# Two direct tiles of batch 1's second layer become a quad of half-size products, in a schedule written by hand

## The chip, the cores and the metric

The kernel runs on one core of a Trainium2 chip. The engines are called as the profile calls them: PE (matmuls), PEld (its weight loads), DVE (vector), ACT (scalar), POOL and SP (the last mostly issues DMAs). The metric is the device time of one execution in microseconds (us); less is better.

## The reference

Four batches of block-sparse attention (8 heads, 768 positions, 64 channels per head, blocks of 32) are followed by a residual MLP over tokens and channels. Cut to what matters:

```python
scores = scale * np.matmul(q, k.transpose(0, 1, 3, 2))
scores = np.where(mask, scores, -1000000000.0)        # window, global and sampled blocks
attn = np.exp(scores - np.max(scores, axis=-1, keepdims=True))
attn = attn / (np.sum(attn, axis=-1, keepdims=True) + 1e-09)
x = np.matmul(attn, v)              # to [4, 768, 512], heads side by side
a1 = alpha1 * x + beta1
tok = np.einsum('ts,bsd->btd', w_tok, a1)              # 768 x 768 over tokens
u = x + lam * tok
a2 = alpha2 * u + beta2
ch = np.maximum(a2 @ w_ch1, 0.0) @ w_ch2               # 512 -> 2048 -> 512
out = u + lam * ch
```

The change touches the last product, `hidden @ w_ch2`, of batch 1: 768 tokens by 2048 hidden channels, times 2048 by 512.

## The kernel before

**Tiling.** Attention goes over 16 pairs of heads (four per batch). A pair is nine units; a unit is one piece of scores (PE, L601, into a PSUM tile), an exponential over it (ACT, L619, into `eT`), a multiplication by the 0/1 mask (DVE, L636), and the products with the values (PE, "PV", L648 and L671, into `op`). A finished pair is divided by its row sums (DVE, L688 and L689) into `x_sb`. POOL then scales `x_sb` for the token mix (L705, L706, `a1pp`), PE mixes tokens (L846), DVE adds (L858) and casts (`ubf`), a transposing DMA on SP's queue brings `ubf` to `uraw` (L898), and DVE scales that to `uT` (L889).

**The channel MLP.** The first layer goes by FFN rows (`job_f1`, L919): four matmuls of 384 columns into an `mm` tile, then a relu on ACT (L926) into one of 16 rows of `hts`. A batch has two halves of 384 tokens, so 32 rows; there are two buffers of `hts`. The second layer has six output tiles of 128 tokens per batch. A *direct* tile is `job_f2` (L1058): 16 matmuls of 512 columns in four jobs of four, into one `mm` tile, then one addition to `x_sb` (DVE, L1067) and a store on SP's queue.

**Quads.** Batches 2 and 3 (`STR = (2, 3)`) take some output tiles in twos, by Strassen's scheme in the form with shared sums: the two tiles are the rows, the two halves of the hidden channels the inner index, and the two halves of the 512 columns the output columns of a 2 × 2 block product. Seven products of half size (`job_p` calling `mul`, L1170: eight matmuls of 256 columns each) stand for the 32 matmuls of 512. They need four sums of activations (`job_s`, DVE, L1144), four differences of `w_ch2`'s quarters (`job_t`, DVE, L1098, 16 instructions in all, once for the kernel), and the accumulations (`plus`, DVE, L1180) into `x_sb`. Products that accumulate in one bank share it: 1, 6 and 5; 7 and 4; 2 and 3 in batch 3.

**PSUM.** Three rings of banks: `mm` (three buffers of one bank), `sp` (two buffers of two banks) and `op` (one). The ring order is that of allocation. A unit group takes two `mm` tiles and two `sp` tiles for its scores.

**Order of work.** After unit 45 the program is emitted from strings written by hand, `WEAVE = W1 + W2 + W2L + W3`, one string per group of three units. Each letter emits one job; the engines run what is emitted in order, each its own. The letters: `q` the scores of three units and the first exponential, `x` the next exponential, `k` the next mask multiplication, `p` the next PV, `f` an FFN row, `g` the next job of the second layer (a direct tile's quarter, or a product), `S` a sum of activations, `A` two rows of the weights' differences, `T` a piece of the token mix, `d` the transposing DMAs, `v` their scaling, `s` the start of a pair's mixing, `0 1 2` jobs of a plan, `K Q Y L` the loads and transpositions of the next pair. `g` and `S` take their jobs in the order of `P_ORDER` and `S_ORDER`. Groups are named p15 to p23 (`W1`), p24 to p35 (`W2`), p36 to p47 (`W2L`) and on. In the kernel before, batch 1 has six direct tiles in order, `A` stands in p29's end, p30 (W2[6]) and p33 (W2[9]).

Of the kernel before, what the change touches and what calls it, by code (L numbers as in the profile page):

```python
# [41 lines left out]
POUR = [-19, 2, 2]  # L42
W1 = [
# [9 lines left out]
]  # L53
W2 = [
# [12 lines left out]
]  # L67
W2L = [
# [18 lines left out]
]  # L87
STR = (2, 3)
HN = NH // 2
HC = DM // 2  # L90
FS = 6
# [157 lines left out]
def kernel(  # L249
# [16 lines left out]
    nc = tc.nc  # L266
# [194 lines left out]
    def sp_tile():  # L461
        return psum.tile([P, 2, 512], FP, name="sp", tag="sp", bufs=2)
# [111 lines left out]
    x_sbs = {}  # L574
# [234 lines left out]
    did = set()  # L809
# [3 lines left out]
    hts = {}  # L813
# [301 lines left out]
    def a_of(b, t, name, r=slice(0, HN)):  # L1115
        if name in ("X1", "X2"):
            return xs[(b, t, name)][:, r]
        c, half = {"11": (0, 0), "12": (0, 1), "21": (1, 0), "22": (1, 1)}[name]
        return hts[(b, c)][:, HN * half + r.start : HN * half + r.stop, ts(t, P)]

    SOP = {
        1: ("X1", "21", "22", ALU.add),
# [5 lines left out]
    def job_s(b, t, n, r=slice(0, HN)):  # L1128
        dst, a, c, op = SOP[n]
        rows = range(r.start, r.stop)  # L1130
        for name in (a, c):
            if name[0] == "X":
                assert all(("S", b, t, int(name[1]), m) in did for m in rows)
            else:
                h, half = divmod(int(name) - 11, 10)
                assert all(("f", b, h, HN * half + m) in did for m in rows)
        if n == 3:
            assert all(("S", b, t, 1, m) in did for m in rows)
        if n == 4:
            assert (b, t, 2) in did  # L1140
        if dst[0] == "X" and (b, t, dst) not in xs:
            tag, bufs = ("eT", 6) if b == B - 1 else ("xs", 4)
            xs[(b, t, dst)] = ap_.tile([P, HN, P], BF, name="xs", tag=tag, bufs=bufs)
        nc.vector.tensor_tensor(  # L1144
            out=a_of(b, t, dst, r), in0=a_of(b, t, a, r), in1=a_of(b, t, c, r), op=op
        )
        did.update(("S", b, t, n, m) for m in rows)
# [8 lines left out]
        7: ("21", "T3", 3),  # L1156
    }
    banks = {}

    def mul(b, t, n, ps, start, cols=slice(0, HC)):  # L1160
        a, m, need = PROD[n]
        assert m in bq or all((m, r) in did for r in range(0, HN, 2))
        if need:
            assert all(("S", b, t, need, r) in did for r in range(HN))
        c, half = {"1": (0, 0), "X": (1, 0)}.get(a[0], (1, 0))
        if need == 0:
            h, half = divmod(int(a) - 11, 10)
            assert all(("f", b, h, HN * half + r) in did for r in range(HN))
        for r in range(HN):
            nc.tensor.matmul(  # L1170
                ps,
                a_of(b, t, a)[:, r],
                b_rows(m, r)[:, 0, cols],
                start=(start and r == 0),
                stop=(r == HN - 1),
                skip_group_check=True,
            )

    def plus(x, ps):
        nc.vector.tensor_tensor(out=x, in0=x, in1=ps, op=ALU.add)  # L1180

    def twice(ps):
        return ps.unsqueeze(1).broadcast_to([P, 2, HC])

    lo, hi = slice(0, HC), slice(HC, DM)

    def job_p(b, t, n):
        x = x_sbs[b]
        last = (b, t) == (B - 1, NT // 2 - 1)
        bk = banks.setdefault((b, t), {})  # L1190
        if n in (1, 2, 7):
            bk[n] = sp_tile()[:, 0] if n == 1 else mm_tile()[:]
        if n == 3 and not last and 2 not in bk:
            bk[2] = mm_tile()[:]
        if n == 1:
            mul(b, t, 1, bk[1][:, lo], True)
            plus(x[:, t, lo], bk[1][:, lo])
        elif n == 2:
            mul(b, t, 2, bk[2][:, lo], True)
            if last or b < B - 1:  # L1200
                plus(x[:, t, lo], bk.pop(2)[:, lo])
            if last:
                emit_store(b, t, lo)
        elif n == 6:
            mul(b, t, 6, bk[1][:, lo], False)
            plus(x[:, t + 3, lo], bk[1][:, lo])
        elif n == 7:
            mul(b, t, 7, bk[7][:, lo], True)
            plus(x[:, t + 3, hi], bk[7][:, lo])
        elif n == 5:  # L1210
            mul(b, t, 5, bk[1][:, lo], False)
            plus(x[:, t : t + 4 : 3, hi], twice(bk[1][:, lo]))
        elif n == 4:
            mul(b, t, 4, bk[7][:, lo], False)
            plus(x[:, t + 3, lo], bk[7][:, lo])
            emit_store(b, t + 3, slice(0, DM))
        elif last:
            for h in range(2):
                sl = slice(HC + h * P, HC + h * P + P)
                ps = (mm_tile(), op_tile([P, DM]))[h]  # L1220
                mul(b, t, 3, ps[:, sl], True, ts(h, P))
                plus(x[:, t, sl], ps[:, sl])
                emit_store(b, t, sl, (nc.sync, nc.scalar)[h])
        else:
            sl = hi if b < B - 1 else slice(0, DM)
            mul(b, t, 3, bk[2][:, hi], b < B - 1)
            plus(x[:, t, sl], bk[2][:, sl])
            emit_store(b, t, slice(0, DM))
        did.add((b, t, n))

    NPAIR = B * NP
# [34 lines left out]
    def start_mlp(b):  # L1266
# [4 lines left out]
        else:  # L1271
            todo["f"] += [
                lambda c=c, n=n: job_f1(b, c, n) for c in range(2) for n in range(NH)
            ]
        if b not in STR:
            todo["g"] += [
# [6 lines left out]
        ]  # L1283
        todo["S"] += [lambda t=t, n=n, r=r: job_s(b, t, n, r) for t, n, r in S_ORDER[b]]

    REST = (6, 7, 5, 4, 3)
    P_ORDER = {
        2: [(0, g, "g") for g in range(4)]
        + [(t, 2) for t in (1, 2)]
        + [(3, g, "g") for g in range(4)]  # L1290
        + [(t, 1) for t in (1, 2)]
        + [(t, n) for t in (1, 2) for n in REST],
        3: [(t, n) for t in range(2) for n in (1, 2)]
        + [(t, n) for t in range(2) for n in REST]
        + [(2, n) for n in (1, 2) + REST],
    }
    ALL, R1, R2 = slice(0, HN), slice(0, HN // 2), slice(HN // 2, HN)
    S_ORDER = {
        2: [(t, n, ALL) for t in (1, 2) for n in (1, 2, 3, 4)],
        3: [(t, n, R1) for n in (1, 2, 3) for t in range(3)]  # L1300
        + [(t, n, r) for t in range(3) for n, r in ((1, R2), (2, R2), (3, R2), (4, ALL))],
    }

    def start_pair(i):
# [227 lines left out]
```

## Time and profile before

| | |
|---|---|
| median of 3 runs | 298.71 us (298.64 to 299.35) |
| profiled execution | 298.76 us, span 297.1 us |
| granted PE clock | 1.000 |
| busy PE | 289.7 us (98%) |
| busy PEld | 193.5 us (65%) |
| busy DVE | 237.8 us (80%) |
| busy ACT | 217.1 us (73%) |
| busy POOL | 109.8 us (37%) |
| second layer, direct (L1058) | 205 records of 128x512 |
| half-size products (L1170) | 128x256, four groups by tile |

The span is from the first instruction to the last; the execution's time adds what lies around it. A row of a group gives line, engine, operation, tiles, count, then busy time and mean duration of one in nanoseconds, then the engine's idle time ahead and what ended it. Matmuls are pipelined: a matmul's duration is longer than its spacing to the next. In a timeline row stand start and length of a stretch of like instructions, in us, their count, and in brackets how long the engine had been idle and what released it. A window row gives the busy time of each engine in that stretch, the PE clock, the DMA share and GB/s.

### The profile page before, as it was taken

What the parts mean: (1) busy time and instruction counts of PE and PEld (TensorE: products, weight loads), DVE (VectorE), ACT (ScalarE), POOL (GpSimd) and SP (SyncE); (2) the same over time, 40 slices, a digit from 0 to 9 for tenths busy, and PEclk for the clock granted to TensorE, in tenths of its full rate; (3) what the DMA queues carried; (4) which work ended last, traced back from release to release, by engine and by line L of the source; (5) the groups of instructions that cost most, each with busy time, mean ns of one, the idle gap of its engine ahead of it and who ended that gap; (6) DMA issues with size and microseconds to landing.
All of it is one profiled execution on the core that took longest, in us unless ns stands there. A gap on an engine that the chain in (4) does not pass through costs nothing.

```text
span 297.1 us, 7554 instructions
## 1 busy us (share of the span) xinstructions
PE 289.7 (98%) x3082; PEld 193.5 (65%) x3101; DVE 237.8 (80%) x485; ACT 217.1 (73%) x324; POOL 109.8 (37%) x149
## 2 busy tenths in 40 slices
PE   8999999999999999999999999999999999999995
PEld 3688888665567565565576466556576679665884
DVE  4988899995678796977878777895956899799774
ACT  4999999998899963999779581999869744576000
POOL 8997978632443710355323340335320300000000
PEclk9999999999999999999999999999999999999999
DMA  6999999992392995729955767745520211400032
GB/s 182 184 199 186 192 171 187 171 123 44 95 147 55 112 203 84 118 65 119 125 96 73 124 110 146 103 92 69 70 62 17 38 38 29 141 1 3 0 141 73
DMA packets 57274, 31.09 MB, mean 105 GB/s; under 512 B 37204, under 2 KB 54016, under 8 KB 57240
## 3 DMA queue, kind: packets, MB, share of 16 engines
q0 software_dynamic: 16752, 14.22, 34.4%
q1 hardware_dynamic: 40020, 15.92, 29.3%
q8 instruction: 24, 0.39, 0.6%
q10 hardware_dynamic: 468, 0.47, 0.5%
q14 instruction: 10, 0.08, 0.1%
HBM read 29.75 MB, written 6.29 MB: 121 GB/s over the span
## 4 chain that ended last, share of the span: by engine, by line
PE 84%; DVE 6%; DMA 4%; ACT 3%; issue 1%; POOL 1%; SPq 0%; POOLq 0%
PE mm L919 18%; PE mm L1058 13%; PE sp L601 10%; PE mm L846 8%; PE op L671 7%; PE mm L1170 5%; PE sp L1170 4%; PE mm L601 3%; DVE eT L636 3%; PE mm L822 3%; PE op L648 2%; DMA vr<-in_v_dram 2%; ACT eT L619 2%; PE mm L1016 2%; PE sp L1016 2%; DMA uraw<-ubf 2%
## 5 line engine op out<-in xcount | busy, mean ns | idle before, releaser
L619 ACT ACTIVATE eT<-sp,expb 128x1024 f16<-128x1024 f32 x111 | 118.4, 1120 | 2.1 <-PE sp L601 1.4
L636 DVE TENSOR_TENSOR eT<-eT,mask 128x1024 f16<-128x1024 f16 x99 | 80.6, 843 | 13.5 <-ACT eT L619 13.3
L919 PE MATMUL mm<-uT,w1b 128*128 128x384 bf16 x416 | 76.8, 326 | 0.4 <-ACT hts L926 0.3
L705 POOL TENSOR_TENSOR a1pp<-x_sb,vbc 128x384 bf16<-128x384 f32 x25 | 28.5, 1138 | 119.0 <-DVE x_sb L689 84.7
L619 ACT ACTIVATE eT<-mm,expb 128x512 f16<-128x512 f32 x66 | 41.7, 685 | 26.5 <-PE mm L601 26.3
L926 ACT ACTIVATE hts<-mm 128x384 bf16<-128x384 f32 x104 | 49.1, 502 | 13.3 <-PE mm L919 12.4
L919 PEld LDWEIGHTS <-w1b 128*128 128x128 bf16 x416 | 38.7, 98 | 26.4 <-issue 2.9
L1058 PE MATMUL mm<-w2b,hts 128*128 128x512 bf16 x205 | 52.2, 379 | 0.9 <-issue 0.2
L671 PEld LDWEIGHTS <-eT 128*128 128x128 f16 x792 | 29.8, 98 | 8.8 <-issue 1.7
L1058 PEld LDWEIGHTS <-hts 128*128 128x128 bf16 x224 | 19.8, 98 | 22.3 <-issue 3.9
L671 PE MATMUL op<-vext,eT 128*128 128x65 f16 x792 | 32.1, 194 | 0.4 <-DVE x_sb L689 0.3
L601 PE MATMUL sp<-qTs,kTs 88*128 88x512 bf16 (+1 forms) x120 | 26.9, 325 | 1.2 <-ACT eT L619 0.7
L706 POOL TENSOR_TENSOR a1pp<-a1pp,vbc 128x384 bf16<-128x384 bf16 x25 | 26.7, 1069 | 2.0
L846 PE MATMUL mm<-a1pp,wtokT 128*128 128x256 bf16 x216 | 25.9, 273 | 0.1
L846 PEld LDWEIGHTS <-wtokT 128*128 128x128 bf16 x216 | 20.6, 98 | 5.6 <-issue 1.8
L1170 PEld LDWEIGHTS <-hts 128*128 128x128 bf16 x208 | 19.5, 98 | 3.0 <-issue 0.3
L858 DVE TENSOR_TENSOR x_sb<-x_sb,mm 128x512 f32<-128x512 f32 x18 | 12.3, 686 | 9.9 <-PE mm L846 9.8
L601 PE MATMUL sp<-qhT,khT 64*128 64x256 bf16 (+1 forms) x176 | 19.8, 322 | 0.0
L601 PEld LDWEIGHTS <-khT 64*128 64x128 bf16 x264 | 10.6, 94 | 12.7 <-issue 9.2
L648 PEld LDWEIGHTS <-eT 128*128 128x128 f16 x360 | 14.9, 97 | 3.8 <-issue 0.3
L689 DVE TENSOR_TENSOR x_sb<-op,rcp 128x384 f32<-128x384 f32 x28 | 15.6, 558 | 1.0
L1067 DVE TENSOR_TENSOR x_sb<-x_sb,mm 128x512 f32<-128x512 f32 x14 | 9.6, 686 | 8.2 <-PE mm L1058 6.7
(135 smaller groups left out, 376.9 us busy)
## 6 DMA issues: line engine op xcount, KB each, us to landing
out_dram<-x_sb SPq DMA_DIRECT2D x23, 256.0 KB
qpad<-in_q_dram POOLq DMA_DIRECT2D x15, 192.0 KB, 4.6
kr<-in_k_dram POOLq DMA_DIRECT2D x15, 192.0 KB, 5.3
vr<-in_v_dram POOLq DMA_DIRECT2D x15, 192.0 KB, 6.3
w1b<-in_moe_w_ch_dram POOLq DMA_DIRECT2D x4, 512.0 KB, 9.2
w2b<-in_moe_w_ch_dram POOLq DMA_DIRECT2D x4, 512.0 KB, 7.7
hts<-in_moe_w_tok_dram POOLq DMA_DIRECT2D x2, 576.0 KB, 8.7
x_sb<-in_k_dram ACTq DMA_DIRECT2D x2, 192.0 KB
```

What stands on the lines that cost most here:

```text
L601: nc.tensor.matmul(sp[jj][:, dst], lhsT, rhs, start=True, stop=True, skip_group_check=True,)
L619: nc.scalar.activation(dst, at, AF.Exp, bias=expb[:], scale=SCALE)
L636: nc.vector.tensor_mul(out=e, in0=e, in1=keep)
L648: nc.tensor.matmul(op[0][:, o, :], ets[u][:, jj, h * QB + n * P : h * QB + n * P + P], vexts[i % NVB][:, w, 2 * jp + jj, :], start=op[1] == 0,
L671: nc.tensor.matmul(op[0][:, o, :], ets[u][:, jj, h * QB + n * P : h * QB + n * P + P], vexts[i % NVB][:, w, 2 * jp + jj, :], start=op[1] == 0,
L705: eng.tensor_tensor(out=dst, in0=x_sbs[b][:, :, cols], in1=bc[0], op=ALU.mult)
L706: eng.tensor_tensor(out=dst, in0=dst, in1=bc[1], op=ALU.add)
L846: nc.tensor.matmul(ps[:, o], wtokT[:, os_, ts(2 * n + o, P)], a1pps[i][:, os_, :], start=(os_ == 0 and o == 0), stop=(os_ == NT - 1 and o ...
L919: nc.tensor.matmul(ps[:, 0:QC], w1b[:, dk, ts(n, P)], uTs[b][:, dk, ts(c, QC)], start=(dk == 0), stop=(dk == 3),)
L926: nc.scalar.activation(h_row(b, c, n), ps[:, 0:QC], AF.Relu)
L1058: nc.tensor.matmul(ps[:], ht[:, nk, ts(o % 3, P)], w2b[:, nk, :], start=(nk == 0), stop=(nk == NH - 1),)
L1170: nc.tensor.matmul(ps, a_of(b, t, a)[:, r], b_rows(m, r)[:, 0, cols], start=(start and r == 0), stop=(r == HN - 1), skip_group_check=True,)
```

## The change

Batch 1's tiles 0 and 1 become a quad; its tiles 2 to 5 stay direct and follow it. `STR` includes batch 1, the order of its second layer is products 2, 1, 6, 5, 7, 3, 4 and then the direct tiles. Tiles of a quad are now given as a pair `(o1, o2)`, since 0 and 1 are not three apart as the pairs of batches 2 and 3 are. Batch 1's product 1 takes an `mm` tile (kept through 6 and 5) in place of an `sp` tile, and product 3 has an `mm` tile of its own. The 16 differences move from p29, p30 and p33 into seven groups of `W1` and the first of `W2`. The FFN rows of batch 1 move forward: p30 has nine in place of seven, p31 six in place of four, and p34, p35 and p36 have none of their two, one and one left. The jobs of the second layer move back. `W2L` and `W3` are the same. The number of sums in `S` rises by four, each over eight rows (128x1024).

```diff
 W1 = [
     "q x L 0 k p f 1 2 f f x p f f f k p K f k",
-    "q Y 0 f 1 k p 2 x f f f x f k k p f g",
+    "q Y 0 f 1 k A A A p 2 x f f f x f k k p f g",
     "q x g f f x 0 k 1 p k g 2 Q k",
-    "q K x g p k 0 k 1 x Q p L Y f f g 2 g k",
-    "q g g x x 0 1 f k 2 k f p k p",
-    "q 0 s 1 s k x x p T f 2 k f k p",
+    "q A A K x g p k 0 k 1 x Q p L Y f f g 2 g k",
+    "q A A A g g x x 0 1 f k 2 k f p k p",
+    "q A A A 0 s 1 s k x x p T f 2 k f k p",
     "q 0 Q 1 k T p x Y k 2 x f p k K",
-    "q f 0 1 x s f T 2 f L d k k x f k f p p",
-    "q 0 x p x g k k 1 d g k g 2",
+    "q f 0 1 x s f T 2 f L d k A k x f k f p p",
+    "q A A 0 x p x g k k 1 d g k g 2",
 ]
 W2 = [
-    "q 0 p p g k x L x p f k 1 K 2 k",
+    "q A A 0 p p g k x L x p f k 1 K 2 k",
...
-    "q k 0 f x f p s f f x 1 L p k 2 f f f k Y A A A A A f",
-    "q f L f 0 f k A A A A A A A A 1 f Y x f p g x f p f g k k 2",
-    "q x k x k Q 0 g 1 s f f g p 2 p f f k p",
-    "q T 0 k f 1 x k f T x f 2 p k K p",
-    "q A A A x 0 x T k 1 k f 2 k f Q f d p L",
-    "q x 0 x K k g d k s f g f 1 k p p g 2",
-    "q Y g x x k g k f 0 1 k 2 p g v g v",
+    "q k 0 f x f p s f f x 1 L p k 2 f f f k Y f",
+    "q f L f 0 f k 1 f f S Y x f p f x f p f k k 2",
+    "q x f k x f k Q 0 1 s f f p 2 p f f k S p",
+    "q T 0 k f 1 x k f T x f 2 p k K p g",
+    "q S S g x 0 x T k g 1 k f 2 k f Q f d p L",
+    "q x 0 x K k g d k s g 1 k p p g 2",
+    "q Y g x x k g k 0 1 k 2 p g v g v",
 ]
...
-STR = (2, 3)
+STR = (1, 2, 3)
...
+    LATE = [(2, (1, 4)), (2, (2, 5))] + [(3, (o, o + 3)) for o in range(3)]
...
     def job_p(b, t, n):
-        x = x_sbs[b]
-        last = (b, t) == (B - 1, NT // 2 - 1)
+        x, (o1, o2) = x_sbs[b], t
+        tail = b == B - 1
+        last = tail and o2 == NT - 1
         bk = banks.setdefault((b, t), {})
-        if n in (1, 2, 7):
-            bk[n] = sp_tile()[:, 0] if n == 1 else mm_tile()[:]
-        if n == 3 and not last and 2 not in bk:
-            bk[2] = mm_tile()[:]
+        if n == 1 and (b, t) in LATE:
+            bk[1] = sp_tile()[:, 0]
+        elif n in (1, 2, 7) or (n == 3 and not tail):
+            bk[n] = mm_tile()[:]
...
+    def direct(*tiles):
+        return [(o, g, "g") for o in tiles for g in range(4)]
+
+    def quad(t, order):
+        return [(t, n) for n in order]
...
     P_ORDER = {
+        1: quad((0, 1), (2, 1, 6, 5, 7, 3, 4)) + direct(2, 3, 4, 5),
...
     S_ORDER = {
+        1: [((0, 1), n, ALL) for n in (1, 2, 3, 4)],
```

What the diff leaves out replaces the arithmetic on one tile number by the pair of tiles, in `a_of`, `mul` and the rest of `job_p`, gathers the checks of readiness in `a_ready`, and writes batches 2 and 3's orders, which stay the same, with `quad` and `direct`. In the changed kernel's numbering `mul`'s matmul is L1169, `plus` L1179 and the sums L1145.

More of the change, by code (lines that the diff above doesn't have):

```diff
@@ L1117, in a_of, with a_ready @@
             return xs[(b, t, name)][:, r]
-        c, half = {"11": (0, 0), "12": (0, 1), "21": (1, 0), "22": (1, 1)}[name]
-        return hts[(b, c)][:, HN * half + r.start : HN * half + r.stop, ts(t, P)]
+        o, half = t[int(name[0]) - 1], int(name[1]) - 1
+        return hts[(b, o // 3)][:, HN * half + r.start : HN * half + r.stop, ts(o % 3, P)]
+    def a_ready(b, t, name, rows):
+        if name[0] == "X":
+            return all(("S", b, t, int(name[1]), m) in did for m in rows)
+        o, half = t[int(name[0]) - 1], int(name[1]) - 1
+        return all(("f", b, o // 3, HN * half + m) in did for m in rows)
     SOP = {
@@ L1130, in job_s @@
         rows = range(r.start, r.stop)
[L1131 to L1136, printed above, removed]
+        assert a_ready(b, t, a, rows) and a_ready(b, t, c, rows)
         if n == 3:
@@ L1164, in mul @@
             assert all(("S", b, t, need, r) in did for r in range(HN))
[L1165 to L1168, printed above, removed]
+        assert a_ready(b, t, a, range(HN))
         for r in range(HN):
@@ L1221, in job_p @@
                 mul(b, t, 3, ps[:, sl], True, ts(h, P))
-                plus(x[:, t, sl], ps[:, sl])
-                emit_store(b, t, sl, (nc.sync, nc.scalar)[h])
-        else:
[L1225 to L1228, printed above, removed]
+                plus(x[:, o1, sl], ps[:, sl])
+                emit_store(b, o1, sl, (nc.sync, nc.scalar)[h])
+        else:
+            assert {(b, t, m) for m in (1, 2, 5)} <= did
+            sl, ps = (slice(0, DM), bk[2]) if tail else (hi, bk[3])
+            mul(b, t, 3, ps[:, hi], not tail)
+            plus(x[:, o1, sl], ps[:, sl])
+            emit_store(b, o1, slice(0, DM))
         did.add((b, t, n))
@@ L1284, in start_mlp @@
         todo["S"] += [lambda t=t, n=n, r=r: job_s(b, t, n, r) for t, n, r in S_ORDER[b]]
+    def direct(*tiles):
+        return [(o, g, "g") for o in tiles for g in range(4)]
+    def quad(t, order):
+        return [(t, n) for n in order]
     REST = (6, 7, 5, 4, 3)
     P_ORDER = {
[L1288 to L1295, printed above, removed]
+        1: quad((0, 1), (2, 1, 6, 5, 7, 3, 4)) + direct(2, 3, 4, 5),
+        2: direct(0)
+        + quad((1, 4), (2,))
+        + quad((2, 5), (2,))
+        + direct(3)
+        + quad((1, 4), (1,))
+        + quad((2, 5), (1,))
+        + quad((1, 4), REST)
+        + quad((2, 5), REST),
+        3: quad((0, 3), (1, 2))
+        + quad((1, 4), (1, 2))
+        + quad((0, 3), REST)
+        + quad((1, 4), REST)
+        + quad((2, 5), (1, 2) + REST),
     }
     ALL, R1, R2 = slice(0, HN), slice(0, HN // 2), slice(HN // 2, HN)
+    Q3 = [(0, 3), (1, 4), (2, 5)]
     S_ORDER = {
-        2: [(t, n, ALL) for t in (1, 2) for n in (1, 2, 3, 4)],
-        3: [(t, n, R1) for n in (1, 2, 3) for t in range(3)]
-        + [(t, n, r) for t in range(3) for n, r in ((1, R2), (2, R2), (3, R2), (4, ALL))],
+        1: [((0, 1), n, ALL) for n in (1, 2, 3, 4)],
+        2: [(t, n, ALL) for t in ((1, 4), (2, 5)) for n in (1, 2, 3, 4)],
+        3: [(t, n, R1) for n in (1, 2, 3) for t in Q3]
+        + [(t, n, r) for t in Q3 for n, r in ((1, R2), (2, R2), (3, R2), (4, ALL))],
     }
```

19 lines of the change are left out of this document (10 added, 9 removed).

## The prediction

> **What bounds the kernel now.** I read the page's share of each engine and its chain first, then a table by stage over the groups that the change touches, then timelines at their seams.
>
> ```profile
> PE 289.7 (98%) x3082; PEld 193.5 (65%) x3101; DVE 237.8 (80%) x485; ACT 217.1 (73%) x324; POOL 109.8 (37%) x149
> PEclk9999999999999999999999999999999999999999
> PE 84%; DVE 6%; DMA 4%; ACT 3%; issue 1%; POOL 1%; SPq 0%; POOLq 0%
> ```
>
> PE is busy for 98% of the span at full clock and holds 84% of the chain that ended last. The table below has a row per group, from the group's first score matmul to the next one's; I write p30 for the group whose text is W2[6], so p34 is W2[10] and p36 is W2L[0].
>
> ```profile
> 134.56:142.44 7.88, 7.83 (x69) 4.49 (x70) 6.16 (x18) 6.76 (x12) 3.40 (x6) 1.00 1.17 141
> 142.44:148.73 6.29, 6.24 (x70) 3.81 (x70) 5.08 (x6) 4.79 (x8) 2.56 (x2) 1.00 1.01 122
> 154.89:159.38 4.49, 4.49 (x47) 3.08 (x45) 3.90 (x10) 4.09 (x8) 0.00 (x0) 1.00 0.00 0
> 159.38:164.88 5.50, 5.45 (x55) 2.94 (x54) 5.26 (x8) 4.42 (x7) 3.83 (x5) 1.00 0.86 115
> 164.88:170.21 5.33, 5.17 (x41) 2.55 (x42) 3.49 (x8) 3.66 (x5) 0.67 (x2) 1.00 0.89 157
> 170.21:173.69 3.48, 3.43 (x54) 2.11 (x54) 2.17 (x4) 3.06 (x4) 3.40 (x5) 1.00 0.05 6
> sum 56.63, PE 56.21 PEld 34.53 DVE 44.57 ACT 41.83 POOL 20.25; mean PE 6.25 PEld 3.84 DVE 4.95 ACT 4.65 POOL 2.25
> ```
>
> Columns: the stretch, its length, then busy PE, PEld, DVE, ACT, POOL. The sum is over nine groups, 127.77 to 184.40 (three not shown). PE is busy for 56.21 of 56.63 us: no wait to remove, so only fewer PE microseconds gain, and each new wait of PE is paid in full. ACT is the runner-up: 6.76 of 7.88 us in p30.
>
> **The change part by part.** *Fewer matmul columns.* Two direct tiles (32 matmuls of 512 columns) become seven products (56 of 256).
>
> ```profile
> 174.44 1.90 PE L1058 MATMUL mm<-w2b,hts 128*128 128x512 bf16 x8
> 232.02 1.04 PE L1170 MATMUL mm<-w2b,hts 128*128 128x256 bf16 x8
> 135.32 3.42 PE L919 MATMUL mm<-uT,w1b 128*128 128x384 bf16 x20
> L1058 PE MATMUL mm<-w2b,hts 128*128 128x512 bf16 x205 | 52.2, 379 | 0.9 <-issue 0.2
> L1170 PE MATMUL mm<-w2b,hts 128*128 128x256 bf16 (+1 forms) x80 | 10.0, 267 | 0.0
> L919 PE MATMUL mm<-uT,w1b 128*128 128x384 bf16 x416 | 76.8, 326 | 0.4 <-ACT hts L926 0.3
> ```
>
> A run of eight takes seven pitches and one duration: (1.90 − 0.379)/7 = 0.217 us at 512 columns, (1.04 − 0.267)/7 = 0.110 at 256; at 384, (3.42 − 0.326)/19 = 0.163. 32 × 0.217 = 6.94 and 56 × 0.110 = 6.16: −0.78 us, all on PE.
>
> The Trainium skill ("TensorE: Matmul & The Clock Gate", section "Back-to-back issue gap") gives about 131 ns for a sustained matmul of 512 columns and 81 for one of 128; by an estimate midway, 98 ns at 256, the quad would cost 56 × 0.098 = 5.5 against 32 × 0.131 = 4.2, or +1.3 us. The two first rows say otherwise (217 and 110 ns), so the sum stays with them.
>
> *Sixteen weight differences (L1098) leave p30 (13) and p33 (3) for the first ten groups.*
>
> ```profile
> 134.42 1.41 DVE L1098 TENSOR_TENSOR qTs<-w2b 128x512 bf16<-128x512 bf16 x4
> L1098 DVE TENSOR_TENSOR qTs<-w2b 128x512 bf16<-128x512 bf16 x4 | 1.4, 409 | 0.0
> 66.25 0.69 DVE L636 TENSOR_TENSOR eT<-eT,mask 128x1024 f16<-128x1024 f16 x1 [0.31 <-ACT eT L619]
> 67.46 0.53 PE L671 MATMUL op<-vext,eT 128*128 128x65 f16 x12
> 75.65 0.69 DVE L1067 TENSOR_TENSOR x_sb<-x_sb,mm 128x512 f32<-128x512 f32 x1 [0.87 <-PE sp L601]
> 82.00 0.69 DVE L1067 TENSOR_TENSOR x_sb<-x_sb,mm 128x512 f32<-128x512 f32 x1 [2.10 <-PE mm L1058]
> 85.66 0.69 DVE L636 TENSOR_TENSOR eT<-eT,mask 128x1024 f16<-128x1024 f16 x1 [1.16 <-ACT eT L619]
> 99.18 0.20 DVE L688 RECIPROCAL rcp<-op 128x6 f32<-128x6 f32 x1 [0.87 <-PE op L671]
> 104.23 0.69 DVE L1067 TENSOR_TENSOR x_sb<-x_sb,mm 128x512 f32<-128x512 f32 x1 [0.94 <-PE mm L1058]
> ```
>
> One costs DVE about 0.335 us ((1.41 − 0.409)/3, with 0.409 the mean of that row's group), 5.4 for all. Each new place stands at a DVE idle time (in brackets): three in p16 where 0.31 is idle, two in p18 at 0.87, three in p19 at 2.10, three in p20 at 1.16, two in p23 at 0.87, two in p24 before 0.94; the single one of p22 has no row here. Only the first overflows, by 3 × 0.335 − 0.31 = 0.70, and its mask product is done at 66.25 + 0.69 = 66.94, 0.5 before the PV that reads it, so 0.2 would show. I take 0, since five of six places hold what they get. Bounds: 0, and 0.7 at each of three places should the idle time lie elsewhere (2.1). Where the differences leave, PE had no wait, so nothing returns. What fills p30's DVE instead is less (6.16 busy falls by about 4), and it doesn't matter.
>
> *Four sums (L1145) and seven accumulations instead of two.*
>
> ```profile
> L1144 DVE TENSOR_TENSOR hts<-hts,xs 128x1024 bf16<-128x1024 bf16 x5 | 3.4, 684 | 0.0
> L1180 DVE TENSOR_TENSOR x_sb<-x_sb,sp 128x512 f32<-128x512 f32 x5 | 3.4, 684 | 0.5 <-PE sp L1170 0.5
> L1180 DVE TENSOR_TENSOR x_sb<-x_sb,mm 128x256 f32<-128x256 f32 x15 | 6.2, 417 | 1.4 <-PE mm L1170 1.4
> ```
>
> These are batch 2's and 3's (by form). Sums 4 × 0.68, accumulations 6 × 0.42 + 0.68 less 2 × 0.69: +4.5 us of DVE in p30 to p37, which has 44.57 busy of 56.63. Free in itself; its queueing is priced in the fourth wait. ACT's relus are the same in number, only earlier; POOL and SP issue the same DMAs, and SP stores batch 1's first two tiles once a product has ended, behind the transposing DMAs, with no reader.
>
> *FFN rows move forward.* p30 goes from 7 rows to 9, p31 from 4 to 6, p34 from 2 to 0, p35 and p36 from 1 to 0; second-layer jobs take their places. PE's sum is unchanged by it, but ACT's and the three `mm` banks' timing isn't. I follow each bank from its user to its next taker.
>
> ```profile
> 158.47 1.27 ACT L926 ACTIVATE hts<-mm 128x384 bf16<-128x384 f32 x3
> 171.79 2.12 ACT L619 ACTIVATE eT<-sp,expb 128x1024 f16<-128x1024 f32 x2
> 170.63 1.27 ACT L619 ACTIVATE eT<-mm,expb 128x512 f16<-128x512 f32 x2 [1.67 <-PE mm L601]
> 159.38 0.40 PE L601 MATMUL mm<-qhT,khT 64*128 64x512 bf16 x2
> 173.91 0.60 PE L601 MATMUL sp<-qhT,khT 64*128 64x256 bf16 x6
> ```
>
> Relus back to back are 0.385 apart and last 0.50; wide exponentials 1.0 apart, 1.12 long; half ones 0.58 apart.
>
> - Wait 1, start of p31. Its second score tile takes the bank of the eighth of p30's nine FFN rows. In p30 ACT has, from the fifth relu on (its matmuls end 4.2 us into the group): relu 0.38, exponential 1.0, relus 0.38 and 0.38, exponential 1.0, relu 0.49: it ends at 7.83. PE arrives at p30's length of 7.88 with two rows more and two jobs of four 512s fewer: 7.88 + 2 × 0.65 − 8 × 0.217 = 7.44. **+0.4** (0.2 to 0.55).
> - Wait 2, in p31: its fourth row takes the bank of its first, whose relu stands behind an exponential on ACT: 0.37 + 2 × 0.58 + 1.0 + 0.50 = 3.03 into the group, where PE has done its scores (0.87) and three rows: 0.87 + 3 × 0.65 = 2.82. **+0.2** (0 to 0.4).
> - Wait 3, start of p34. Products 1, 6 and 5 hold one `mm` bank, so the score tile waits for the last FFN relu of p33 and no longer for the one before. The row of three relus ends at 159.74, PE arrives at 159.38: 0.36, less up to 0.1 for the tile's place within its pair: **+0.28** (0.2 to 0.4).
> - Wait 4, start of p35. The second score tile takes the bank of product 3, whose eight matmuls are the last of p34; before, a direct tile's bank stayed open across the seam. DVE must add it first.
>
> ```profile
> 161.10 3.35 DVE L636 TENSOR_TENSOR eT<-eT,mask 128x1024 f16<-128x1024 f16 x3 [0.21 <-ACT eT L619]
> 167.31 1.99 DVE L636 TENSOR_TENSOR eT<-eT,mask 128x1024 f16<-128x1024 f16 x3
> 160.97 1.00 POOL L705 TENSOR_TENSOR a1pp<-x_sb,vbc 128x384 bf16<-128x384 f32 x1 [9.22 <-DVE x_sb L689]
> 162.05 1.25 POOL L706 TENSOR_TENSOR a1pp<-a1pp,vbc 128x384 bf16<-128x384 bf16 x1
> ```
>
> With DVE idle: the last matmul's duration beyond its pitch (0.267 − 0.110) and the add's 0.417, **0.57**. But p34's DVE has three mask products, 3.35 us while POOL computes against 1.99 without, and now two further additions ahead of it: by this the backlog is 0.6 more, **+1.17**; with a second stretched product 1.9. I take 1.17, since those POOL operations come at this place. The Trainium skill ("SBUF — State Buffer", "Who interferes with whom") has the two share a port with exclusive use, which these rows bear out.
>
> - Wait 5, p36 to p37. Without its FFN row p36 is 0.65 us shorter for PE (4 × 0.163), while ACT still has four exponentials from 170.63 to 171.79 + 2.12 = 173.91, and PE's scores into `sp` began at 173.91, of which the second tile, 0.2 later, takes the bank of the last exponential. 0.65 − 0.2: **+0.45** (0.3 to 0.5).
>
> Cover gone at each: the FFN matmuls that stood between a relu and the next score tile. After p37 the program is as before.
>
> Sum: −0.78 + 0 + 0.4 + 0.2 + 0.28 + 1.17 + 0.45 = +1.72. The profiled execution took 298.76 with its span of 297.1, 0.05 above the median 298.71. Forecast 298.71 + 1.72 = **300.4 us**.
>
> **The rivals.**
>
> - *No new wait (the other side).* One condition decides: DVE and ACT are done with a bank when PE comes to it at every seam, as in all of the shown groups before, where PE lost 0.42 in nine. For it: ACT is busy for only 41.83 of 56.63 us, DVE for 44.57. Against: the walks above are by order, not by load. Time 298.71 − 0.78 = 297.9.
> - *Waits at their low ends.* DVE is idle when product 3 ends and the rest absorb one another: −0.78 + 0.2 + 0 + 0.2 + 0.57 + 0.3 = +0.49, or 299.2. From p30 on DVE loses 4 us of differences, which speaks for it.
> - *The early differences delay the mask products.* Three places are overrun by the 0.7 of the first, which keeps 0.2 after its PV's margin while the two others keep 0.5 each: 300.4 + 1.2 = 301.6. Against: the idle times above.
> - *Half-size matmuls are no cheaper.* A pitch above 6.94/56 = 0.124 us turns the gain around; a tenth of a 512's 0.217 above half of it, 0.130, would make +0.3 instead of −0.78: 301.5. The 0.110 row speaks against.
>
> **How the numbers follow.** Forecast 0.50 (own range 299.6 to 301.2), low ends 0.20, no wait 0.10, early differences 0.12, half-size 0.03, something not seen 0.05. The forecast, the low ends and the early differences hold 0.82, so the range goes from the low ends less 0.3 to 301.7, a little over the early differences: 298.9 to 301.7. No change is what lies within 0.3% (0.9 us; about what a measurement can tell): 297.8 to 299.6. Forecast: slower 0.48, same 0.02. Low ends: same 0.17, slower 0.03. No wait: same 0.06, faster 0.04. Early differences and half-size: slower 0.15. Unseen: faster 0.02, same 0.01, slower 0.02. Together faster 0.06, same 0.26, slower 0.68.
>
> **What would show it.** The pitch of products in p32 to p35 at 0.110; no PE wait before 130 us and DVE idle shorter at the six places; PE waits with releaser ACT `hts` at the starts of p31 and p34, DVE `x_sb` (L1180's successor) at p35, and ACT `eT` at p37. Wrong if the p35 wait is under 0.6 (low ends) or if PE waits on DVE `eT` in the first ten groups.

## The result and the profile after

The changed kernel takes 299.80 us (median of 5 runs, 299.72 to 300.55) against 298.70 us before (298.62 to 299.35). The ratio of the runs is 1.0049 with a 95% interval of 1.0037 to 1.0062: slower, and by 1.1 us between the medians. The forecast was 300.4 in a range of 298.9 to 301.7. The profiled execution took 299.72 with a span of 298.0, against 298.76 and 297.1. One execution of all that follow (306.47 us in run 9, at a granted clock of 0.989) is left out of the medians and ratios.

The first table is the groups p29 to p37 of the changed kernel (five of the nine rows and their sum), each from its first score matmul to the next one's (length, then busy PE, PEld, DVE, ACT, POOL); the rows answer to those of the prediction, with the new start times.

```profile
134.54:141.98 7.44, 7.44 (x69) 4.47 (x68) 2.26 (x5) 6.72 (x13) 3.37 (x5) 1.00 1.12 144
141.98:148.50 6.52, 6.39 (x69) 3.97 (x68) 5.48 (x7) 6.22 (x13) 2.61 (x2) 1.00 1.14 115
161.87:166.35 4.48, 4.48 (x59) 3.48 (x57) 3.62 (x8) 3.50 (x5) 3.43 (x4) 1.00 0.79 95
166.35:171.71 5.36, 4.96 (x42) 2.65 (x42) 3.78 (x9) 3.27 (x4) 0.96 (x2) 1.00 1.07 194
171.71:174.53 2.82, 2.82 (x49) 1.85 (x48) 2.06 (x4) 2.40 (x4) 2.31 (x3) 1.00 0.10 32
sum 58.06, PE 57.22 PEld 37.25 DVE 42.22 ACT 41.96 POOL 20.29; mean PE 6.36 PEld 4.14 DVE 4.69 ACT 4.66 POOL 2.25
```

The nine groups take 58.06 us in place of 56.63: +1.43, while their first matmul stands at 127.75 in place of 127.77. So everything ahead of them, with the 16 differences in it, costs nothing. A busy PE isn't a PE at work: the two score matmuls at 141.98, one of which waits for a bank, read 0.83, the two at 155.55 0.39. So the waits are read from the spacing of the rows. At a seam without a wait the next job starts 0.75 us after the first score matmul (155.55 to 156.30 below).

PE's rows of the changed kernel at the seams (start, length, tiles, count):

```profile
141.98 0.83 PE L601 MATMUL mm<-qhT,khT 64*128 64x512 bf16 x2
143.18 2.99 PE L919 MATMUL mm<-uT,w1b 128*128 128x384 bf16 x16
146.01 0.90 PE L671 MATMUL op<-vext,eT 128*128 128x65 f16 x24
...
155.55 0.39 PE L601 MATMUL mm<-qhT,khT 64*128 64x512 bf16 x2
...
156.30 1.05 PE L1169 MATMUL mm<-w2b,hts 128*128 128x256 bf16 x8
...
161.87 0.65 PE L601 MATMUL mm<-qhT,khT 64*128 64x512 bf16 x2
...
162.89 1.05 PE L1169 MATMUL mm<-qTs,xs 128*128 128x256 bf16 x8
...
165.39 1.04 PE L1169 MATMUL mm<-w2b,hts 128*128 128x256 bf16 x8
166.35 0.28 PE L601 MATMUL mm<-qhT,khT 64*128 64x256 bf16 x1
167.03 0.38 PE L601 MATMUL mm<-qhT,khT 64*128 64x256 bf16 x3 [0.40 <-DVE x_sb L1179]
...
167.77 1.05 PE L1169 MATMUL mm<-kTs,hts 128*128 128x256 bf16 x8
...
174.53 0.39 PE L601 MATMUL mm<-qhT,khT 64*128 64x512 bf16 x2
...
175.46 0.39 PE L601 MATMUL sp<-qhT,khT 64*128 64x512 bf16 x2 [0.31 <-ACT eT L619]
175.78 1.90 PE L1058 MATMUL mm<-w2b,hts 128*128 128x512 bf16 x8
```

All five waits are there: p31 starts 143.18 − 141.98 − 0.75 = 0.45 late; its first four rows take 146.01 − 143.18 = 2.83 in place of 2.60 (16 pitches of 0.163), so 0.23; p34 loses 162.89 − 161.87 − 0.75 = 0.27; p35 167.77 − 166.35 − 0.75 = 0.67; p37 175.78 − 174.53 − 0.75 = 0.50. In sum 2.12. With −0.78 that is +1.34 of the +1.43 measured; the last 0.09 I can't place. A product of eight has the length 1.05, the 1.04 of the kernel before.

Behind p37 some of it comes back. The rows are p38 to p40 together, of the kernel before and then of the changed one:

```profile
sum 12.34, PE 11.98 PEld 6.40 DVE 10.12 ACT 10.70 POOL 3.93; mean PE 3.99 PEld 2.13 DVE 3.37 ACT 3.57 POOL 1.31
```

```profile
sum 11.92, PE 11.92 PEld 6.49 DVE 10.32 ACT 10.69 POOL 4.23; mean PE 3.97 PEld 2.16 DVE 3.44 ACT 3.56 POOL 1.41
```

0.42 us less: in the kernel before a PV in p40 waits, behind a division on DVE, for a scaling that waits for its transposing DMA. The first fence below is the kernel before, the second the changed one.

```profile
192.81 0.48 DVE L889 TENSOR_SCALAR uT<-uraw,ab2T 128x768 bf16<-128x768 bf16 x1 [0.62 <-DMA uraw<-ubf]
195.25 0.91 PE L671 MATMUL op<-vext,eT 128*128 128x65 f16 x24 [0.25 <-DVE x_sb L689]
```

```profile
193.14 0.86 DVE L889 TENSOR_SCALAR uT<-uraw,ab2T 128x768 bf16<-128x768 bf16 x2
196.24 0.90 PE L671 MATMUL op<-vext,eT 128*128 128x65 f16 x24
```

1.43 − 0.42 = 1.01, and the profiled executions differ by 0.96.

### The profile page after: what moved, and what is told of

It is laid out like the page before. It is cut to its first block, busy times and chain, and to the rows that moved or that the text cites. A ratio compares the mean times of both kernels' runs of the same rounds, so it can differ in the third digit from the quotient of the medians.

```text
span 298.0 us, 7632 instructions
## 1 busy us (share of the span) xinstructions
PE 291.4 (98%) x3125; PEld 196.2 (66%) x3125; DVE 241.3 (81%) x494; ACT 217.1 (73%) x324; POOL 109.7 (37%) x149
## 4 chain that ended last, share of the span: by engine, by line
PE 86%; ACT 6%; DVE 4%; issue 1%; DMA 1%; ACTq 0%
PE mm L919 21%; PE mm L1058 13%; PE sp L601 11%; PE mm L846 8%; PE op L671 7%; PE mm L1169 6%; ACT eT L619 4%; PE sp L1169 4%; PE mm L601 3%; PE mm L822 3%; PE op L648 2%; PE mm L1016 2%; PE sp L1016 2%; DVE eT L636 2%; PE mm L648 1%; ACT hts L926 1%
## 5 line engine op out<-in xcount | busy, mean ns | idle before, releaser
L636 DVE TENSOR_TENSOR eT<-eT,mask 128x1024 f16<-128x1024 f16 x99 | 79.5, 828 | 14.6 <-ACT eT L619 14.5
L705 POOL TENSOR_TENSOR a1pp<-x_sb,vbc 128x384 bf16<-128x384 f32 x25 | 28.5, 1139 | 120.1 <-DVE x_sb L689 86.2
L1058 PE MATMUL mm<-w2b,hts 128*128 128x512 bf16 x192 | 46.6, 380 | 0.0
L1058 PEld LDWEIGHTS <-hts 128*128 128x128 bf16 x192 | 17.0, 97 | 18.7 <-issue 2.8
L706 POOL TENSOR_TENSOR a1pp<-a1pp,vbc 128x384 bf16<-128x384 bf16 x25 | 26.7, 1069 | 2.0
L1169 PEld LDWEIGHTS <-hts 128*128 128x128 bf16 x248 | 23.1, 98 | 4.1 <-issue 1.1
L601 PE MATMUL sp<-qhT,khT 64*128 64x256 bf16 (+1 forms) x176 | 20.5, 323 | 0.3 <-ACT eT L619 0.3
L858 DVE TENSOR_TENSOR x_sb<-x_sb,mm 128x512 f32<-128x512 f32 x18 | 12.3, 686 | 10.1 <-PE mm L846 10.1
L601 PE MATMUL mm<-qhT,khT 64*128 64x512 bf16 (+1 forms) x88 | 13.9, 330 | 0.5 <-DVE x_sb L1179 0.4
```

The costliest lines, as they stand in the source:

```text
L601: nc.tensor.matmul(sp[jj][:, dst], lhsT, rhs, start=True, stop=True, skip_group_check=True,)
L636: nc.vector.tensor_mul(out=e, in0=e, in1=keep)
L705: eng.tensor_tensor(out=dst, in0=x_sbs[b][:, :, cols], in1=bc[0], op=ALU.mult)
L706: eng.tensor_tensor(out=dst, in0=dst, in1=bc[1], op=ALU.add)
L1058: nc.tensor.matmul(ps[:], ht[:, nk, ts(o % 3, P)], w2b[:, nk, :], start=(nk == 0), stop=(nk == NH - 1),)
L1169: nc.tensor.matmul(ps, a_of(b, t, a)[:, r], b_rows(m, r)[:, 0, cols], start=(start and r == 0), stop=(r == HN - 1), skip_group_check=True,)
```

## The experiments

Theory A is the prediction's, with the five waits as measured: the quad gains 0.78, the early differences cost nothing, and every wait comes from where a row or a product was put.

**1. The early differences alone.** The kernel before with only this:

```diff
+ the A's of W1[1], [3], [4], [5], [7], [8] and W2[0] as in the change
- the A's of W2[5], W2[6] and W2[9]
```

> The kernel before with only the sixteen weight differences moved to the first ten groups. Theory A (they fill DVE idle time, and PE didn't wait where they stood): 298.7, no new PE wait before 130 us, within 0.2 of before. Rival B (they push mask products past their PV): 299.0 or more, with PE waits on DVE eT between 65 and 105 us.

Measured: 298.79 against 298.68, ratio 1.0008 (0.9999 to 1.0017), and no row of PE brackets a wait from 60 to 108 us. (The new places are six groups of `W1` and the first of `W2`, seven in all.) The one place that I had reckoned as overrun (p16) reads so in the changed kernel:

```profile
65.50 1.09 DVE L1098 TENSOR_TENSOR qTs<-w2b 128x512 bf16<-128x512 bf16 x3
66.85 0.68 DVE L636 TENSOR_TENSOR eT<-eT,mask 128x1024 f16<-128x1024 f16 x1
```

The mask product comes 0.60 later than before (66.25), and PE's next group starts 0.02 later than before (69.45 against 69.43). Theory A holds.

**2. The differences late, the rest as changed.** The A's back in W2[5], [6] and [9].

> The changed kernel with the differences back where the kernel before has them (end of p29, p30, p33). Theory A: PE's five new waits don't come from them, 299.8 within 0.2, with the same waits of 0.45, 0.23, 0.27, 0.67 and 0.50 us. Rival B (they cost something in the first groups): 299.5 or less. A third way, that thirteen differences in p30 hold up the sums for the products: 300.2 or more with a PE wait in p32 or p33.

Measured: 299.91, ratio 1.0038 (1.0026 to 1.0051), with the same five waits and one of 0.17 more in p33, ahead of product 6 (the third way that was expected, but small). So the move of the differences costs nothing in either schedule, and helps by no more than that.

**3. Product 3 ahead of 7.**

```diff
-        1: quad((0, 1), (2, 1, 6, 5, 7, 3, 4)) + direct(2, 3, 4, 5),
+        1: quad((0, 1), (2, 1, 6, 5, 3, 7, 4)) + direct(2, 3, 4, 5),
```

> The changed kernel with the order 2, 1, 6, 5, 3, 7, 4: product 7, whose bank stays with product 4, is now the last before the seam at p35, and product 3's bank is added one product earlier. Theory A (the wait at p35 is the addition of product 3 ahead of the score tile that takes its bank): the wait of 0.67 falls to 0.1 or less; time 299.1, or up to 299.5 where the wait at p40 (0.43 before, none in the changed kernel) comes back. Rival C (the DVE backlog of p34 is what counts, whatever the bank): the wait stays at 0.5 or more and the time at 299.8.

Measured: 299.19, ratio 1.0014 (1.0005 to 1.0022). The wait at p35 is gone and the other four are as they were: in this schedule the bank of the last product before the seam is the whole of it (run 6 has the same order and waits at p35 again, since DVE is later there).

**4. Rows as before, products where direct jobs stood.** FFN rows, and the g's of p30 to p36, as in the kernel before; `direct(2)` ahead of the quad, whose order is the third run's; one g less in p37.

> The quad, the early differences and four sums as in the change, but FFN rows stand as in the kernel before (p30 has 7, p31 4, p34 2, p35 1, p36 1), the four direct jobs in p30 and p31 stay (tile 2's), the products come in p34 and p35 where direct jobs stood, and one second-layer job less in p37. Theory A (the quad itself gains 0.78, the waits came from where rows and products were put): no PE wait over 0.3 in p30 to p37, 297.9, or 297.5 if the wait at p40 stays away. Rival D (a quad at this place always meets PSUM or DVE waits that eat it): 298.7 or more.

Measured: 300.30, ratio 1.0057 (1.0043 to 1.0070): a miss for theory A. The waits of p31 are gone, but three come inside p34 and p35 and one at p37 (0.3, 0.5, 1.3 and 0.6). The largest is product 4 behind product 7, which it accumulates on; DVE's rows show what 7's addition stood behind:

```profile
169.54 0.38 PE L1169 MATMUL mm<-tmore,hts 128*128 128x256 bf16 x2
171.10 1.03 PE L1169 MATMUL mm<-kTs,hts 128*128 128x256 bf16 x8 [1.18 <-DVE x_sb L1179]
```

```profile
168.74 1.29 DVE L636 TENSOR_TENSOR eT<-eT,mask 128x1024 f16<-128x1024 f16 x2
169.94 0.19 DVE L688 RECIPROCAL rcp<-op 128x6 f32<-128x6 f32 x1
170.16 0.56 DVE L689 TENSOR_TENSOR x_sb<-op,rcp 128x384 f32<-128x384 f32 x1
170.64 0.41 DVE L1179 TENSOR_TENSOR x_sb<-x_sb,mm 128x256 f32<-128x256 f32 x1
```

Product 7 ends at 169.92; its addition comes at 170.64, behind two mask products and a division. Direct quarters need nothing from DVE between them, accumulating products do: seven products in two groups can't stand where seven direct jobs stood.

**5. The rows forward, without a quad.** The kernel before with all letters of the change but S, and the 24th direct job in p37.

> The kernel before with every letter where the change has it (early differences, FFN rows forward, fewer second-layer jobs in p30 and p31), but with batch 1's six tiles direct, no quad and no sums; the 24th direct job goes to p37. Theory A (waits 1, 2 and 5 come from the rows alone, waits 3 and 4 from the quad's banks): waits of 0.45 at p31, 0.23 in p31 and 0.5 at p37, none over 0.3 at p35; with 0.78 not saved and the wait at p40 gone, 298.7 + 1.2 - 0.2 to 0.4 = 299.5 to 299.7. Rival (the waits need the quad): 298.7.

Measured: 300.73 against 298.91, ratio 1.0056 (1.0031 to 1.0081). The waits at p31 (0.46), in p31 (0.23) and at p37 (0.5) are there without any quad, and none at p35: as expected. The time isn't, by 1 us, for two reasons. The wait at p34 is there too:

```profile
162.80 0.65 PE L601 MATMUL mm<-qhT,khT 64*128 64x512 bf16 x2
163.82 1.90 PE L1058 MATMUL mm<-w2b,hts 128*128 128x512 bf16 x8
```

163.82 − 162.80 − 0.75 = 0.27 without a product: a direct tile's bank that is held over that seam does it as well. And the wait at p40 is larger, not gone (0.71 by the spacing, of which the row brackets 0.55). With both, 0.46 + 0.23 + 0.27 + 0.50 + 0.71 − 0.42 = 1.75, against 1.82 between the medians. (The profiled execution is the longest of the five, 301.80; it had lost 0.9 at 17 us, where PE waits for a load, ahead of all this.)

**6. One row left for p36.** As the third run, and W2[9] ends `2 k f Q d p L` in place of `2 k f Q f d p L`.

> The run with product 3 ahead of 7, and one FFN row of p33 (its last) left for p36. Theory A: the wait at p37 (0.50) goes because p36 has its 0.65 us of PE work again beside ACT's four exponentials, and the wait at p34 (0.27) goes because the relu that the score tile needs is older: 299.2 - 0.7 = 298.5. Rival (ACT is late at p37 because p34 to p36 push it, whatever PE does): the wait at p37 stays at 0.4 or more, 299.0 or more.

Measured: 299.09 where 298.5 was expected; the ratio falls from the third run's 1.0014 only to 1.0010 (0.9999 to 1.0021). The wait at p37 is gone, so its cause was right. The wait at p34 (0.27) isn't: the last of two rows stands as close to the seam as the last of three. And p35 waits again, 0.66 in all, for product 3's addition and then for 7's: with a row less in p33, p34's first mask product starts with POOL's first operation (163.10 and 163.07) and takes 1.52 in place of 0.80, of which more in run 8.

**7. Products a group apart.** Rows as before; product 2 in p32, 1 and 6 in p33, 5, 3, 7 in p34, 4 in p35.

> All rows where the kernel before has them; four direct jobs of tile 2 in p30 and p31; products 2 in p32, 1 and 6 in p33, 5, 3 and 7 in p34, 4 in p35 between two direct jobs of tile 3; three direct jobs fewer in p37. Each product that accumulates stands a group away from the one before it, and the last before a seam is not one that the next group's tiles wait for. Theory A (0.78 is there, and every wait comes from a place): no PE wait over 0.3 in p30 to p37, 297.9 (297.5 where the wait at p40 goes too). Rival D (a quad here always meets waits that eat it): 298.7 or more.

Measured: 300.18, ratio 1.0044 (1.0029 to 1.0059): a miss. With product 1's bank held and direct tile 3's over p36, the FFN rows between them have too few banks. PE's rows that bracket a wait:

```profile
163.45 0.81 PE L919 MATMUL mm<-uT,w1b 128*128 128x384 bf16 x4 [0.34 <-ACT eT L619]
166.78 0.81 PE L919 MATMUL mm<-uT,w1b 128*128 128x384 bf16 x4 [0.77 <-DVE x_sb L1179]
170.30 1.02 PE L1058 MATMUL mm<-w2b,hts 128*128 128x512 bf16 x4 [0.34 <-ACT eT L619]
178.14 0.37 PE L601 MATMUL mm<-qhT,khT 64*128 64x512 bf16 x1 [0.27 <-ACT hts L926]
```

So the moving of the rows ahead of the products, which makes waits 1, 2 and 5, also keeps rows and products off each other's banks.

**8. Exponentials earlier.** The changed kernel, with

```diff
-    "q f L f 0 f k 1 f f S Y x f p f x f p f k k 2",
-    "q x f k x f k Q 0 1 s f f p 2 p f f k S p",
+    "q f x L f 0 f k f x 1 f f S Y f p f f p f k k 2",
+    "q f x k f x k Q 0 1 s f f p 2 p f f k S p",
```

> The changed kernel with only the two wide exponentials of p30 and of p31 emitted earlier among the FFN rows (same rows, same products). Theory A (waits 1 and 2 are relus queued behind an exponential on ACT): both go (0.45 and 0.23), the other three stay: 299.8 - 0.6 = 299.2. Rival (ACT is simply too full in p30 and p31, 6.7 of 7.4 us, whatever its order): the waits only move, 299.7 or more.

Measured: 302.06, ratio 1.0106 (1.0084 to 1.0129). The edit does more than was meant: p30's new string has ten `f`, not nine, so p33 is left with two rows. The wait at p31's start is gone; in p31 0.19 is lost at its last two rows in place of 0.23 at its fourth. But p30 itself stalls. ACT's rows:

```profile
137.65 1.27 ACT L926 ACTIVATE hts<-mm 128x384 bf16<-128x384 f32 x3
140.67 1.11 ACT L619 ACTIVATE eT<-sp,expb 128x1024 f16<-128x1024 f32 x1 [1.74 <-PE op L671]
141.68 1.87 ACT L926 ACTIVATE hts<-mm 128x384 bf16<-128x384 f32 x4
```

The second exponential takes an `eT` buffer that the next PV frees, and that PV stands on PE behind FFN rows (now seven, before six) whose relus are behind the exponential. And p35's wait has doubled, from 0.67 to 1.39. DVE's and POOL's rows of p34 and PE's at p35, in this run, and then DVE's and POOL's in the changed kernel:

```profile
165.03 1.52 DVE L636 TENSOR_TENSOR eT<-eT,mask 128x1024 f16<-128x1024 f16 x1
166.47 0.68 DVE L1179 TENSOR_TENSOR x_sb<-x_sb,mm 128x512 f32<-128x512 f32 x1
168.73 0.41 DVE L1179 TENSOR_TENSOR x_sb<-x_sb,mm 128x256 f32<-128x256 f32 x1
165.00 1.00 POOL L705 TENSOR_TENSOR a1pp<-x_sb,vbc 128x384 bf16<-128x384 f32 x1 [11.29 <-DVE x_sb L689]
169.19 0.38 PE L601 MATMUL mm<-qhT,khT 64*128 64x256 bf16 x3 [1.13 <-DVE x_sb L1179]
```

```profile
163.59 0.80 DVE L636 TENSOR_TENSOR eT<-eT,mask 128x1024 f16<-128x1024 f16 x1 [0.83 <-ACT eT L619]
166.57 0.41 DVE L1179 TENSOR_TENSOR x_sb<-x_sb,mm 128x256 f32<-128x256 f32 x1
162.84 1.00 POOL L705 TENSOR_TENSOR a1pp<-x_sb,vbc 128x384 bf16<-128x384 f32 x1 [11.31 <-DVE x_sb L689]
```

Here the mask product starts with POOL's first operation and takes 1.52; there it starts 0.75 after it and takes 0.80. In both it ends 0.55 behind POOL's operation (166.55 and 166.00; 164.39 and 163.84). What stands behind it on DVE comes 0.72 later, and 0.67 + 0.72 is the 1.39. That decides between the low and the middle price of the prediction's fourth wait, and what decides it is p33's rows: in both traces the product comes 1.7 after p34's first score matmul, but with two rows in p33 PE is there 0.65 earlier, while POOL still follows DVE's division. Runs 2, 3 and 10 have three rows and 0.79 to 0.80, runs 6, 11 and 12 two rows and 1.52.

**9. All seams at once.** The eighth run's strings, the third's order, product 6 after p33's last row, products 5 and 3 together, one g from p37 to p36.

> As the run with exponentials earlier, and also: order 2, 1, 6, 5, 3, 7, 4; product 6 after p33's last FFN row; products 5 and 3 ahead of the later two mask products in p34; one direct job moved from p37 to p36. Theory A (all five waits are matters of place): none over 0.25 left in p30 to p37, 298.7 - 0.78 - up to 0.4 for the wait at p40 = 297.5 to 298.0, faster than both kernels. Rival D (each wait removed lets PE run into the next limit, DVE's adds or ACT's four exponentials): new waits of 0.5 or more in sum, 298.5 or more.

Measured: 302.35 (301.55 to 302.67), ratio 1.0109 (1.0082 to 1.0136). A miss: the tenth row and the `eT` stall of run 8 are in it, p35 waits 0.70, and the largest new wait (1.6 at p37) is taken up with run 11. The wait at p34 is gone (0.01), now that product 6 stands between p33's last row and the seam, though 0.29 is lost in p33 in its place.

**10. PV ahead of the exponential.** The third run, with

```diff
-    "q f L f 0 f k 1 f f S Y x f p f x f p f k k 2",
+    "q f x L f 0 f k f p x 1 f S Y f f p f f k k 2",
```

and p31's string of run 8.

> The run with product 3 ahead of 7 (299.2), and in p30 the first PV moved ahead of the second wide exponential, which comes after the fourth FFN row; in p31 the first wide exponential after the first row. The eT buffer that the exponential takes is then read and free before ACT reaches it. Theory A (waits 1 and 2 are relus behind an exponential, and the 1.7 us stall of the run with exponentials earlier was the eT ring): no stall over 0.3 in p30, none at p31; waits 3 and 5 (0.27, 0.5) stay; 299.2 - 0.6 = 298.6, with the p35 wait between 0 and 0.6. Rival D (the time won is met again at the next seam): a wait of 0.5 or more at p35 and 299.1 or more.

Measured: 298.59 against 298.61, ratio 1.0001 (0.9991 to 1.0010). No stall in p30, none at p31's start, none at p35; those at p34 (0.27) and p37 (0.5) stay, and 0.19 at p31's last two rows as in run 8. With the order of a few letters the change is no slower than the kernel before.

**11. The second try for the rest.** Run 10 with the row for p36 of run 6, and

```diff
-    "q x 0 x K k g d k s g 1 k p p g 2",
+    "q x 0 x K k g g d k s 1 k p p g 2",
```

with product 4 after tile 2's first quarter.

> As the run with PV ahead of the exponential, and also one FFN row of p33 left for p36, products 5 and 3 together ahead of p34's later mask products, and product 4 in p35 after a direct job instead of first. Theory A: waits at p31, p34, p35 and p37 all under 0.3, 297.7 to 298.2. Rival D: waits of 0.5 or more in sum remain at p34 to p37, 298.5 or more.

Measured: 301.34, between 298.80 and 303.03; ratio 1.0089 (1.0055 to 1.0124). SP's, DVE's and PE's rows show what came in:

```profile
165.05 0.34 SPq L1071 DMA_DIRECT2D out_dram<-x_sb  x1
165.43 1.36 SPq L898 DMA_TRANSPOSE uraw<-ubf  x1
```

```profile
175.09 0.48 DVE L889 TENSOR_SCALAR uT<-uraw,ab2T 128x768 bf16<-128x768 bf16 x1 [4.13 <-DMA uraw<-ubf]
176.21 0.53 PE L601 MATMUL mm<-qhT,khT 64*128 64x512 bf16 x1 [2.12 <-DVE x_sb L1067]
```

Product 3, now early, also stores its tile early, ahead of a transposing DMA (`d`). That DMA lands 175.09 − 165.43 = 9.7 us after its issue. Run 9 has the same order and 9.1 (168.13 to 177.25).

The profiled execution (302.46) is one of the longer ones, and its stall costs more than its length. After 2.1 us without PE work the granted clock reads 0.54 from 176.20 to 177.50 and 0.61 from there to 180.33, then 1.00 again. The scores and two direct jobs take 4.11 us there (176.22 to 180.33), 2.26 in run 12 (174.01 to 176.27). The idle times of runs 4, 8 and 9 (1.2 to 1.5 us) left the clock at 1.00. Of the nine executions the four above 302 have a mean clock of 0.992 to 0.994, the others 0.998 to 0.999.

**12. The transposing DMA ahead of the store.** Run 11, and in p34 `g d g` in place of `g g d`.

> The run of the second try with one letter moved: in p34 the transposing DMA of the second half pair is issued after product 5 and ahead of product 3, so that it no longer stands behind product 3's store of 256 KB on SP's queue. In the second try it landed 9.7 us after its issue and DVE waited 4.1 us for it, PE 2.4 us at p37. Theory E (the store ahead of it on the queue, with the loads running, made it late): it lands within 5 us of its issue, the stall at p37 goes, the spread of the runs falls under 1 us, and the time is 298.1 to 298.5 with 0.4 left at p35. Rival F (the loads alone make it late, whatever the order on SP's queue): the landing stays at 8 us or more and the time above 300.

Measured: 298.29 (297.97 to 298.56) against 298.57, ratio 0.9990 (0.9981 to 0.9999). The stall at p37 and the spread are gone:

```profile
163.10 1.30 SPq L898 DMA_TRANSPOSE uraw<-ubf  x1
165.13 8.79 SPq L1071 DMA_DIRECT2D out_dram<-x_sb  x3
170.56 1.55 DVE L889 TENSOR_SCALAR uT<-uraw,ab2T 128x768 bf16<-128x768 bf16 x2
166.38 1.02 PE L1058 MATMUL mm<-w2b,hts 128*128 128x512 bf16 x4 [0.34 <-ACT eT L619]
```

The scalings run without a wait, so it has landed in under 8 us; whether within 5 isn't shown. It is now issued 2.3 us earlier as well, ahead of the store and of the loads, so this run alone doesn't say which of the two had made it late. Other traces narrow it. In p39 of the kernel before and of runs 1 and 5 the same DMA is issued right behind a store with no load on its way, and DVE starts on it 4.6, 4.4 and 4.9 us later (188.19 to 192.81 in the kernel before); in p35 of run 5 it is behind a store with the loads running: 7.5 (166.32 to 173.80). So a store ahead doesn't do it alone; what the loads do alone isn't shown.

This version is the fastest that was run, by the medians 1.5 us below the changed kernel and 0.1% below the one before, with an interval that just leaves out 1. But p30 to p37 take 49.89 in it and 49.84 in the kernel before (first score matmul of p30 to that of p38): 0.19 in p31, 0.27 at p34 and 0.41 at p35 still eat the quad's 0.78. What it wins stands in p38 to p40, 11.92 in place of 12.34.

## Why the prediction was right, and where not

The direction and the mechanism were right, the size was 0.6 too large: 299.8 lies halfway between the forecast of 300.4 and the low-ends rival's 299.2. Two errors of one sign make it, 0.50 in the fourth wait and 0.42 behind p37; the other four waits came out 0.12 larger in sum than forecast. That no wait was there to remove is right too, but busy time doesn't show it; the spacing does, with 0.75 to 0.77 at the seams of p30 to p37 before (at p35, 0.98, a matmul record is missing).

- *Fewer columns, −0.78.* Right: products still have the length 1.05 in their new place. The sustained spacings of the Trainium skill ("TensorE: Matmul & The Clock Gate", section "Back-to-back issue gap"), by which the quad would have been dearer, are not what these traces show (0.217 us at 512 columns, 0.110 at 256).
- *Early differences, 0.* Right, by runs 1 and 2. The rival with 301.6 fell.
- *Waits 1, 2, 3 and 5.* 0.45, 0.23, 0.27 and 0.50 against 0.4, 0.2, 0.28 and 0.45. The cause of 1 is shown by runs 5 and 10, that of 5 by runs 5 and 6. Wait 2 needs no quad either (run 5), but moving the exponential only moved it (0.19 in run 10). The third's cause was told too narrowly: by run 5 it needs a held second-layer bank, not product 1. That the last row's relu is what it waits for fits runs 6 and 9: it stays where that row stays next to the seam's PV, and goes where a product comes between.
- *Wait 4, 1.17.* This term was mis-sized: 0.67. The step that failed is "I take 1.17, since those POOL operations come at this place". They do, but in the changed kernel the mask product had waited for ACT and started 0.75 after POOL's first operation, so it took 0.80 and not 1.4, and DVE had a backlog of only 0.10 when product 3 ended (its addition starts at 166.57, 0.14 after the product's end at 165.39 + 1.04; product 4's, for which DVE was idle, starts 0.04 after). 0.57 + 0.10 = 0.67: the low end was nearly the price. The 0.6 of backlog was worked out from no row. That such a backlog is real shows in run 8 (0.72 more, 1.39 in all): it needs p33 to have two rows and not three.
- *"After p37 the program is as before."* The program is, the time wasn't: p38 to p40 got back 0.42, since the PV of p40 no longer waits for a transposing DMA. Of the profiled runs, those with six direct tiles have that wait at 0.42, 0.19 and 0.71, and the ones with a quad don't; why the DMA lands sooner there isn't settled.

−0.78 + 0.45 + 0.23 + 0.27 + 0.67 + 0.50 − 0.42 = +0.92 is the sum as it should have been, against 0.96 between the profiled executions and 1.1 by the medians.

Rival D, that a quad at this place meets waits that eat it, held by its times for runs 4, 7, 9 and 11. By the times of runs 10 and 12 it fell, but not by their traces: their waits in p30 to p37 sum to 0.96 and 0.87, and no run here has less than 0.78. Run 5 shows that most of these come with the FFN rows' move and not with the quad; a schedule that has the quad and not these waits was not found.

## What to carry to other kernels

Where PE is busy for 98% and its accumulators have three banks, a saving in matmul columns is only worth what the seams leave of it: for each stage, name the bank that its first tile takes, who frees it last, and what that engine has queued ahead. Read the waits from the spacing of matmuls, group by group, and not from the total, which here hides that the last version gains behind the changed groups. Products that accumulate on each other need DVE between them where direct pieces need nothing, so they stand apart, and the last one before a seam should be one whose bank is kept anyway. When a product moves, its store moves too: look at what it is then ahead of on the DMA queue.

## What the runs showed of the hardware that I had not expected

- A mask product on DVE that starts while a POOL operation runs ends 0.54 to 0.56 us behind that operation, wherever it started: 1.52 long when it starts with POOL's L705 (run 8), 1.23 when 0.32 behind (run 9), 0.80 when 0.75 behind (changed kernel), 0.68 alone. An addition from PSUM isn't stretched: 0.68 at 164.31 in the changed kernel, while POOL's L706 runs from 163.92 to 165.17.
- A transposing DMA issued right behind a 256 KB store took 9.7, 9.1 and 7.5 us until DVE could start on it with loads running (runs 11, 9 and 5), 4.4 to 4.9 without (p39). The executions of run 11 spread over 4.2 us (298.80 to 303.03), those of run 12, with the DMA ahead of the store, over 0.6 (297.97 to 298.56).
- PE idle for 2.1 us was followed by a granted clock of 0.54 to 0.61 for 4.1 us (run 11); idle times of 1.2 to 1.5 us were not (runs 4, 8 and 9).
